# Six steps of the first group's second layer as whole fp32 products, with a new order of loads, transposes and lead-in

## Chip, core and metric

The kernel runs on one core of one Trainium2 chip. The metric is the time of one execution on the device, in microseconds (us).

## What is computed

Windowed attention with block summaries feeds a two-layer network:

```python
k_sum = k.reshape(B, H, nb, block, D).max(axis=3)      # B=4, H=8, S=768, D=64, block 32
v_sum = v.reshape(B, H, nb, block, D).mean(axis=3)
scores_l_m = np.where(mask_l, scores_l, -1e9)          # |i - j| < 16
scores_all = np.concatenate([scores_l_m, scores_s], axis=-1)
... softmax a ...
x = matmul(a, v_all)            # laid out as 3072 tokens x 512
h = x @ w_in                    # 2048 hidden units
g = h * np.tanh(softplus(h))    # Mish
out = g @ w_out                 # 3072 x 512
```

## The kernel before

**Groups and steps.** The 3072 tokens are six groups of 512 (`TG`). A group has 16 steps, one for each 128 of the 2048 hidden units, and 96 steps run one after the other. Step i multiplies `ph` = w_in x (line 425, into PSUM), ScalarE forms `a` = Mish(ph) (line 432), and two steps later `po` += a w_out (line 453), in four PSUM tiles of 128 tokens. PE does steps as ph(i), then what there is of attention, then po(i-2).

**Split operands.** x, a and both weights are fp32 values that are split into a high part rounded to fp32r (a 32-bit format that PE takes in one instruction) and a low part, the rest. Each fp32 product is three: high by high, low by high and high by low. So ph is 12 instructions of 128x512 and po another 12. The first group's `ah` is cast on ScalarE (line 441), its `al` subtracted on VectorE (line 443).

**Attention.** A chunk is 256 tokens, and a unit is one chunk of one pair of heads. The 16 turns of scores stand at the steps in the table `at` (0, 4, 8, 12, 15, 19, ...), with two units each. A turn runs over several steps: scores (`sc`, line 330) at its step; row minima and masks on VectorE (`pr`, `nm`, line 352), exps on ScalarE (line 356), reciprocals on VectorE and the multiplication on GpSimd (POOL, line 370) at the next; transposes on PE (`pt_ps`, line 378) at the end of the step after that, with ScalarE's copies (`pt`, line 380); and the products with the values (`x_ps`, line 410) at the next turn. From the turn at step 15 on, the transposes are VectorE's (line 391). VectorE also takes the block maxima of the keys (`km`, line 255, from `ks`) and the block sums of the values (`vq`, line 283, from `vsum`). `ks` and `vsum` share one buffer, so each is loaded when the one before has been reduced.

**Weights.** w_in and w_out reach the core as 16 pieces of two steps each, in the order w_in 0, w_in 2, w_out 0, w_in 4, w_out 2, w_in 6, ... , w_in 14, w_out 12, w_out 14 (a piece is named by its first step, and the order listing prints w_8 for both w_in's and w_out's). They come as 64-bit numbers and are rebuilt as fp32 on the chip. A piece passes through: `load_weight` (SP's queue, two staging buffers); `begin_weight` (ScalarE forms `f`, line 140, by `rebase_weight`, in some steps later than the rest; VectorE forms `x`, lines 144 and 146); `join_weight` (VectorE, lines 154 and 156); `upper_weight` (ScalarE casts `w_hi`, line 164); `lower_weight` (VectorE subtracts `w_lo`, line 171). All of this happens in the lead-in and the first group. SP's queue issues loads in order, and a load whose buffer is not free holds those behind it.

**Lead-in.** Ahead of step 0 a loop over u = 0 to 10 does the attention of the first group's two chunks, a unit at a time, with the first weight pieces between.

**Order.** The program runs under a manual schedule: each engine executes its instructions in the order in which the code is written. Only semaphores tie engines together. The edits lie in the weight helpers (`home`, `begin_weight`, `join_weight`, `upper_weight`), in `ff_act`, `ff_split`, `ff_out`, in the lead-in loop and in the main loop.

## Time and profile before

| | |
|---|---|
| median of 3 runs | 637.01 us (636.95 to 637.9) |
| profiled execution | 634.93 us, span 633.1 us |
| mean granted TensorE clock | 0.987 |
| PE busy | 604.3 us (95%) |
| VectorE (DVE) busy | 384.2 us (61%) |
| ScalarE (ACT) busy | 259.6 us (41%) |
| GpSimd (POOL) busy | 75.6 us (12%) |

The span is cut from the first to the last instruction; the execution's own time is a little longer. In timelines a row gives start, duration, engine, line, operation, output and inputs with their sizes. A bracket holds the idle time ahead of it on its engine and what ended it. PE's matmul ends are modelled: a 128x512 instruction is printed with 0.39 us, but the next one starts 0.227 us later, so that an idle time in a bracket after such an instruction is 0.16 us short. SPq is SP's queue as it issues transfers.

### The profile page before, as it was taken

How to read it: one execution, taken by the hardware profiler on the slowest of the kernel's cores; microseconds unless marked ns; L12 is line 12 of the kernel's file. 1: busy time of each engine (PE TensorE's matmuls, PEld its weight loads, DVE VectorE, ACT ScalarE, POOL GpSimd, SP SyncE). 2: the span in 40 equal slices, each digit the busy share in tenths (PEclk: the TensorE clock that was granted, in tenths of full speed). 3: DMA queues.
4: the chain of work that ended last, by engine and by line, in shares of the span. 5: the costliest groups of instructions: out<-in, count | busy, mean ns of one | idle time of the engine just before them, and what ended most of it. 6: DMA issues, size and time to landing. Idle time of an engine off the chain costs nothing.

```text
span 633.1 us, 10821 instructions
## 1 busy us (share of the span) xinstructions
PE 604.3 (95%) x4104; PEld 494.1 (78%) x4104; DVE 384.2 (61%) x1032; ACT 259.6 (41%) x634; POOL 75.6 (12%) x123
## 2 busy tenths in 40 slices
PE   4768999899999999999999999999999999999997
PEld 3547877688888888788888888888888888888886
DVE  4668999884755667856646658757647536222211
ACT  3759786767245145144143253153253241111111
POOL 4441010112011011010110110110110110000000
PEclk9969999899999999999999999999999999999999
DMA  9946686633134043632033241532232110100001
GB/s 286 329 153 226 228 286 236 217 122 97 67 96 115 9 147 89 199 98 97 0 97 96 91 142 56 173 98 80 83 97 68 30 33 0 67 0 1 1 0 66
DMA packets 31779, 69.26 MB, mean 109 GB/s; under 512 B 4720, under 2 KB 11120, under 8 KB 31728
## 3 DMA queue, kind: packets, MB, share of 16 engines
q1 hardware_dynamic: 31728, 68.58, 34.2%
q8 instruction: 32, 0.52, 0.3%
q14 instruction: 19, 0.16, 0.1%
HBM read 60.16 MB, written 6.29 MB: 105 GB/s over the span
## 4 chain that ended last, share of the span: by engine, by line
PE 82%; DVE 7%; DMA 5%; issue 3%; ACT 1%; POOL 1%; SPq 1%; POOLq 0%; DVEq 0%; ACTq 0%
PE po L453 38%; PE ph L425 38%; PE x_ps L410 3%; DMA vw<-vw 3%; PE sc L330 3%; DMA w<-w_in 1%; DVE w_lo L171 1%; DVE x L144 1%; DVE x L146 1%; DMA ks<-kt 1%; DVE f L154 1%; DVE al L443 1%; DVE km L255 1%; DVE pt L391 1%; DVE pr L352 1%
## 5 line engine op out<-in xcount | busy, mean ns | idle before, releaser
L432 ACT ACTIVATE a<-ph 128x512 f32<-128x512 f32 x96 | 57.3, 597 | 283.8 <-PE ph L425 230.3
L425 PE MATMUL ph<-xh,w_hi 128*128 128x512 f32 x384 | 151.5, 395 | 1.4 <-DVE nm L352 1.4
L453 PE MATMUL po<-w_hi,ah 128*128 128x512 f32 x384 | 151.9, 396 | 0.2 <-DVE o L461 0.2
L425 PE MATMUL ph<-xh,w_lo 128*128 128x512 f32 x384 | 150.9, 393 | 0.0
L425 PE MATMUL ph<-xl,w_hi 128*128 128x512 f32 x384 | 150.8, 393 | 0.0
L453 PE MATMUL po<-w_lo,ah 128*128 128x512 f32 x384 | 149.6, 390 | 0.0
L453 PE MATMUL po<-w_hi,al 128*128 128x512 f32 x384 | 149.5, 389 | 0.0
L441 DVE CAST ah<-a 128x512 fp32r<-128x512 f32 x80 | 34.7, 434 | 144.1 <-ACT a L432 143.6
L391 DVE STREAM_TRANSPOSE pt<-pr 32x256 f32<-32x256 f32 x256 | 111.5, 436 | 3.6
L425 PEld LDWEIGHTS ph<-xh,w_hi 128*128 128x128 f32 x384 | 73.0, 190 | 17.2 <-issue 2.0
L453 PEld LDWEIGHTS po<-w_hi,ah 128*128 128x128 f32 x384 | 72.0, 188 | 18.0 <-issue 3.0
L425 PEld LDWEIGHTS ph<-xh,w_lo 128*128 128x128 f32 x384 | 72.9, 190 | 15.4
L425 PEld LDWEIGHTS ph<-xl,w_hi 128*128 128x128 f32 x384 | 72.9, 190 | 15.1
L453 PEld LDWEIGHTS po<-w_lo,ah 128*128 128x128 f32 x384 | 72.1, 188 | 15.4
L453 PEld LDWEIGHTS po<-w_hi,al 128*128 128x128 f32 x384 | 72.1, 188 | 14.4
L356 ACT ACTIVATE pr<-pr,nm 128x120 f32<-128x120 f32 x192 | 73.2, 382 | 21.1 <-DVE nm L352 20.9
L370 POOL TENSOR_TENSOR pr<-pr,rs 128x960 f32<-128x960 f32 (+1 forms) x28 | 44.0, 1573 | 227.2 <-DVE rs L367 149.1
L443 DVE TENSOR_TENSOR al<-a,ah 128x512 fp32r<-128x512 f32 x96 | 66.6, 694 | 6.5 <-ACT ah L441 3.7
L410 PEld LDWEIGHTS x_ps<-pt,vw 120*64 120x64 f32 x768 | 26.0, 143 | 17.2 <-issue 7.8
L413 DVE TENSOR_TENSOR xl<-x_ps,xh 128x512 fp32r<-128x512 f32 (+1 forms) x28 | 17.2, 614 | 36.2 <-ACT xh L412 35.8
L410 PE MATMUL x_ps<-pt,vw 120*64 120x64 f32 x768 | 29.8, 231 | 8.4 <-POOL pr L370 3.4
L356 ACT ACTIVATION_READ_ACCUMULATOR pr<-pr,nm 128x1 f32 x192 | 35.9, 187 | 0.0
(64 smaller groups left out, 451.4 us busy)
## 6 DMA issues: line engine op xcount, KB each, us to landing
qk<-qk SPq DMA_DIRECT2D x40, 496.0 KB, 4.0
vw<-vw SPq DMA_DIRECT2D x48, 192.0 KB, 5.9
w<-w_in SPq DMA_DIRECT2D x16, 512.0 KB, 3.8
w<-w_out SPq DMA_DIRECT2D x16, 512.0 KB, 4.7
ks<-kt SPq DMA_DIRECT2D x16, 384.0 KB, 4.2
out<-o SPq DMA_DIRECT2D x24, 256.0 KB, 2.3
vsum<-vs SPq DMA_DIRECT2D x12, 384.0 KB, 3.3
vw<-vm SPq DMA_DIRECT2D x40, 48.0 KB
```

The lines of the kernel that those rows point to most:

```text
L144: nc.vector.tensor_scalar(out=half[:, :, 0], in0=quarter[:, :, 1], scalar1=13, scalar2=None, op0=ALU.logical_shift_right)
L330: nc.tensor.matmul(ps[h][row, at0:at0 + KA], u["qk"][r, s, h * QT:(h + 1) * QT], u["qk"][r, s, P:], start=True, stop=True)
L356: nc.scalar.activation(pr[:, j, :], pr[:, j, :], AF.Exp, scale=-1.0, bias=nm[:, j:j + 1], accum_out=sm[:, j:j + 1])
L370: nc.gpsimd.tensor_mul(u["pr"], u["pr"], rs.unsqueeze(2).broadcast_to([P, n, KA]))
L391: nc.vector.transpose(u["tr"][b * SQ:(b + 1) * SQ, :, a * SQ:(a + 1) * SQ], u["wide"][a * SQ:(a + 1) * SQ, :, b * SQ:(b + 1) * SQ])
L410: nc.tensor.matmul(x, u["v"][:, s, d], pt, start=True, stop=True)
L413: return lambda: nc.vector.tensor_sub(xl, x, xh.bitcast(F32))
L425: nc.tensor.matmul(ph, w[:, cc * P:(cc + 1) * P], x[:, cc, :], start=(cc == 0 and n == 0), stop=(cc == NCC - 1 and n == 2))
L432: nc.scalar.activation(a, st[g, fc], AF.Mish)
L441: (nc.scalar.copy if g == 0 else nc.vector.tensor_copy)(ah, a)
L443: return lambda: nc.vector.tensor_sub(al, a, ah.bitcast(F32))
L453: nc.tensor.matmul(po[g][t], a[:, tok], w, start=(fc == 0 and n == 0), stop=(fc == NFC - 1 and n == 2))
```

## The change

- `WHOLE = 6`: in steps 0 to 5 of the first group `a` is written as fp32 and not split. `ff_out` makes one fp32 product for each of the four token tiles in place of three fp32r products, with the fp32 values of w_out pieces 0, 2 and 4.
- Those three pieces are not cast or split when they are joined, but kept, and split at the end of the first group for the later groups: the list `kept` goes to the cast's queue at step 14. Their split starts with one more ScalarE copy each.
- Lead-in: the casts at u = 8 and 10 become one at u = 9, the second split moves from u = 9 to 10, a begin with its load from u = 6 to 7, and the split, join, begin and load that stood between lead-in and step 0 are gone.
- Main loop: PE's transposes move from the end of step i+2 to step i+3, right behind its `ph`. In the first group, the key loads of a turn come one step later. Step 8 joins, begins and loads no weight piece.

```diff
--- before.py
+++ after.py
@@ -43,6 +43,7 @@
 WP = 512
 WB = 2
 SQ = 32
+WHOLE = 6
 
 
 OFFSET = 112
@@ -100,6 +101,8 @@
     weights = sorted(((w, fc) for fc in range(0, NFC, WB) for w in range(2)), key=lambda p: (p[1] + WB * p[0], p[0]))
     NW = len(weights)
     order = {piece: j for j, piece in enumerate(weights)}
+
+    whole = {order[1, fc] for fc in range(0, WHOLE, WB)}
     late = []
     split = {}
 
@@ -111,10 +114,13 @@
         pool = const if j < EARLY else late[0]
         return pool.tile([P, WB * WP], dtype, tag=f"w{part}_{j}", name=name, bufs=1)
 
+    def value_home(j, name):
+        return home(j if j in whole else min(k for k in range(j + 1, NW + 1) if k not in whole), 1, F32, name)
+
     def weight(w, part, fc):
         return split[w, fc - fc % WB, part][:, fc % WB * WP:(fc % WB + 1) * WP]
 
-    loaded, rebases, begun, joined, raised = [], [], [], [], []
+    loaded, rebases, begun, joined, raised, kept = [], [], [], [], [], []
 
     def load_weight():
         if weights:
@@ -136,7 +142,7 @@
             high = flat.bitcast(U32).rearrange("p (f two) -> p f two", two=2)[:, :, 1]
             quarter = flat.bitcast(U16).rearrange("p (f four) -> p f four", four=4)
             x = home(j, 0, U32, f"x{w}_{fc}")
-            f = home(j + 1, 1, F32, f"f{w}_{fc}")
+            f = value_home(j, f"f{w}_{fc}")
             rebases.append(lambda: nc.scalar.activation(f, high.bitcast(F32), AF.Copy, scale=2.0 ** -OFFSET))
             if not wait:
                 rebase_weight()
@@ -155,11 +161,19 @@
                                     op0=ALU.max, op1=ALU.min)
             nc.vector.scalar_tensor_tensor(out=u, in0=u, scalar=3, in1=x,
                                            op0=ALU.logical_shift_left, op1=ALU.bitwise_or)
-            joined.append((w, fc, f))
+            if order[w, fc] in whole:
+                split[w, fc, 2] = f
+                kept.append((w, fc, f))
+            else:
+                joined.append((w, fc, f))
 
     def upper_weight():
         if joined:
             w, fc, f = joined.pop(0)
+            if order[w, fc] in whole:
+                value = f
+                f = home(NW, 1, F32, f"f{w}_{fc}")
+                nc.scalar.copy(f, value)
             split[w, fc, 0] = home(order[w, fc], 0, F32R, f"w{w}_{fc}_hi")
             nc.scalar.copy(split[w, fc, 0], f)
             raised.append((w, fc, f))
@@ -428,12 +442,17 @@
 
     def ff_act(g, fc):
 
-        a = ff.tile([P, TG], F32, tag="t", name=f"a{g}_{fc}", bufs=2)
+        if g == 0 and fc < WHOLE:
+            a = ff.tile([P, TG], F32R, tag="ah", name=f"a{g}_{fc}").bitcast(F32)
+        else:
+            a = ff.tile([P, TG], F32, tag="t", name=f"a{g}_{fc}", bufs=2)
         nc.scalar.activation(a, st[g, fc], AF.Mish)
         st[g, fc] = a
 
     def ff_split(g, fc):
 
+        if g == 0 and fc < WHOLE:
+            return lambda: None
         a = st[g, fc]
         ah = ff.tile([P, TG], F32R, tag="ah", name=f"ah{g}_{fc}")
         al = ff.tile([P, TG], F32R, tag="al", name=f"al{g}_{fc}")
@@ -443,13 +462,17 @@
         return lambda: nc.vector.tensor_sub(al, a, ah.bitcast(F32))
 
     def ff_out(g, fc):
-        ah, al = st.pop((g, fc))
+        a = st.pop((g, fc))
         if fc == 0:
             po[g] = [ps_o.tile([P, DM], F32, tag="o", name=f"po{g}_{t}") for t in range(TG // P)]
-        wh, wl = (weight(1, part, fc) for part in range(2))
+        if g == 0 and fc < WHOLE:
+            products = ((a, weight(1, 2, fc)),)
+        else:
+            wh, wl = (weight(1, part, fc) for part in range(2))
+            products = ((a[0], wh), (a[1], wh), (a[0], wl))
         for t in range(TG // P):
             tok = slice(t * P, (t + 1) * P)
-            for n, (a, w) in enumerate(((ah, wh), (al, wh), (ah, wl))):
+            for n, (a, w) in enumerate(products):
                 nc.tensor.matmul(po[g][t], a[:, tok], w,
                                  start=(fc == 0 and n == 0), stop=(fc == NFC - 1 and n == 2))
             if fc == NFC - 1:
@@ -510,12 +533,13 @@
             first_key_summary(u + 1)
         if lower:
             lower()
-        if u in (3, 9):
+        if u in (3, 10):
             lower_weight()
         if u in (2, 8, 10):
             join_weight()
+        if u in (2, 9):
             upper_weight()
-        if u in (1, 6, 8, 10):
+        if u in (1, 7, 8, 10):
             begin_weight()
             load_weight()
         if u == 1:
@@ -530,12 +554,8 @@
 
     turns = sorted(at)
     values = dict(zip(turns[1:] + [turns[-1] + 4], (at[i] for i in turns)))
-    turned = {i + 2: group for i, group in at.items() if i < NFC - 1}
+    turned = {i + 3: group for i, group in at.items() if i < NFC - 1}
     following = dict(zip(turns, (at[i] for i in turns[1:])))
-    lower_weight()
-    join_weight()
-    begin_weight()
-    load_weight()
     for i in range(len(steps) + 2):
         if i - 1 in at and i < NFC:
             att_normalize(at[i - 1])
@@ -544,6 +564,8 @@
             ff_act(*steps[i])
             if i < NFC:
                 split_rest = ff_split(*steps[i])
+            if i in turned:
+                att_transpose(turned[i])
         if i - 1 in at:
             upper_weight()
             rebase_weight()
@@ -577,24 +599,31 @@
         if i in following:
             n, m = following[i]
             att_summarize_keys(*n)
-            for unit in (n, m):
-                att_load_keys(*unit)
+            if i >= NFC - 1:
+                for unit in (n, m):
+                    att_load_keys(*unit)
         if i - 1 in following:
             n, m = following[i - 1]
             if i >= NFC:
                 att_summarize_values(*n)
             if m[0] % CPB == 0:
                 load_key_source(m[0] // CPB, m[1])
+            if i < NFC:
+                for unit in (n, m):
+                    att_load_keys(*unit)
         if i - 2 in following:
             n, m = following[i - 2]
             att_summarize_keys(*m)
             for unit in (n, m):
                 att_block_keys(*unit)
+        if i == NFC - 2:
+            joined.extend(kept)
         if i not in at:
             upper_weight()
-        join_weight()
-        begin_weight(i in at)
-        load_weight()
+        if i != NFC // 2:
+            join_weight()
+            begin_weight(i in at)
+            load_weight()
         if i not in at:
             lower_weight()
         if i - 1 in at:
@@ -604,8 +633,6 @@
                 att_load_values(*unit)
         if i >= 2:
             ff_out(*steps[i - 2])
-        if i in turned:
-            att_transpose(turned[i])
 
 
 # ---- launch: one core ----
```

**Places where instructions move.** The first is ScalarE at lead-in turn u = 7, where `f_2` rebases w_out's piece, `pr_3` are the exps of the last unit, and the copies and casts feed PE. Before:

```order
L380 COPY pt_0_573<-pt_ps_0_574 120x512
L140 ACTIVATE f_2_582<-w_2_170 128x1024
L356 ACTIVATE pr_3_607,sm_3_609<-pr_3_607,nm_3_608 128x120 x4
L412 CAST xh_380<-x_ps_0_622 128x256
L380 COPY pt_1_633<-pt_ps_1_634 120x512
```

and with the change:

```order
L394 COPY pt_0_573<-pt_ps_0_574 120x512
L370 ACTIVATE pr_3_599,sm_3_601<-pr_3_599,nm_3_600 128x120 x4
L426 CAST xh_380<-x_ps_0_614 128x256
L394 COPY pt_1_625<-pt_ps_1_626 120x512
L146 ACTIVATE f_2_634<-w_2_170 128x1024
```

The exps of the last unit and the transposes' copy now stand ahead of the rebase.

The second is VectorE around step 8, where `w_8_lo` out of f_8_1115 (before) and f_8_1086 (now) is the low part of w_out's piece 8. Before, with the first row of step 8's masks last:

```order
L154 TENSOR_SCALAR f_12_1168<-f_12_1168 128x1024
L156 SCALAR_TENSOR_TENSOR f_12_1168<-f_12_1168,x_12_1167 128x1024
L144 TENSOR_SCALAR x_10_1232<-w_10_1119 128x1024
L146 TENSOR_SCALAR x_10_1232<-w_10_1119 128x1024
L171 TENSOR_TENSOR w_8_lo<-f_8_1115,w_8_hi 128x1024
L352 ISA pr_0_1308,nm_0_1309<-sc_0_0_1290,first 128x120
```

and with the change, behind the masks and `xl` of step 8:

```order
L462 TENSOR_TENSOR al_8_1172<-a_8_1169,ah_8_1171 128x512
L269 TENSOR_REDUCE km_2_1231<-ks_2_1136 128x24
L380 TENSOR_SCALAR rs_0_1253<-sm_0_1212 128x8
L381 RECIPROCAL rs_0_1253<-rs_0_1253 128x8
L297 TENSOR_REDUCE vq_2_1278<-vsum_2_1233 96x32
L298 TENSOR_SCALAR vq_2_1278<-vq_2_1278 96x32
L462 TENSOR_TENSOR al_9_1273<-a_9_1270,ah_9_1272 128x512
L160 TENSOR_SCALAR f_12_1143<-f_12_1143 128x1024
L162 SCALAR_TENSOR_TENSOR f_12_1143<-f_12_1143,x_12_1142 128x1024
L150 TENSOR_SCALAR x_10_1291<-w_10_1090 128x1024
L152 TENSOR_SCALAR x_10_1291<-w_10_1090 128x1024
L185 TENSOR_TENSOR w_8_lo<-f_8_1086,w_8_hi 128x1024
```

The low part of w_out 8 stood ahead of step 8's masks and stands at the end of step 9 now, behind `km_2`, `vq_2` and a join and a begin.

The third is VectorE at steps 10 to 14, where `w_14_lo` out of f_14_1340 (before) and f_14_1343 (now) is the low part of w_in's piece 14. Before, from step 10 to step 11:

```order
L443 TENSOR_TENSOR al_10_1438<-a_10_1435,ah_10_1437 128x512
L255 TENSOR_REDUCE km_3_1441<-ks_3_1395 128x24
L154 TENSOR_SCALAR f_12_1402<-f_12_1402 128x1024
L156 SCALAR_TENSOR_TENSOR f_12_1402<-f_12_1402,x_12_1401 128x1024
L144 TENSOR_SCALAR x_14_1451<-w_14_1343 128x1024
L146 TENSOR_SCALAR x_14_1451<-w_14_1343 128x1024
L171 TENSOR_TENSOR w_14_lo<-f_14_1340,w_14_hi 128x1024
L443 TENSOR_TENSOR al_11_1499<-a_11_1496,ah_11_1498 128x512
```

and with the change, in step 13 and the start of step 14:

```order
L381 RECIPROCAL rs_2_1523<-rs_2_1523 128x8
L462 TENSOR_TENSOR al_13_1543<-a_13_1540,ah_13_1542 128x512
L160 TENSOR_SCALAR f_14_1502<-f_14_1502 128x1024
L162 SCALAR_TENSOR_TENSOR f_14_1502<-f_14_1502,x_14_1501 128x1024
L185 TENSOR_TENSOR w_14_lo<-f_14_1343,w_14_hi 128x1024
L185 TENSOR_TENSOR w_12_lo<-f_12_1406,w_12_hi 128x1024
L462 TENSOR_TENSOR al_14_1589<-a_14_1586,ah_14_1588 128x512
```

The low part of w_in 14 stood at the end of step 11 and stands at the end of step 13 now, behind the join of w_out's piece 14.

## Rows read from the trace of the kernel before

**Rows 1.** The page, busy time of each engine, its share of the span and its instructions.

```profile
PE 604.3 (95%) x4104; PEld 494.1 (78%) x4104; DVE 384.2 (61%) x1032; ACT 259.6 (41%) x634; POOL 75.6 (12%) x123
```

**Rows 2.** Busy time in two stretches of 16 us, in the first group and in the second. Columns: stretch, its length, busy us (and instructions) of PE, PEld, DVE, ACT, POOL, granted clock, DMA share, GB/s.

```profile
64.00:80.00 16.00, 16.00 (x126) 13.12 (x125) 15.82 (x30) 12.53 (x21) 0.00 (x0) 1.00 0.70 236
...
144.00:160.00 16.00, 16.00 (x129) 13.18 (x128) 5.87 (x24) 9.56 (x25) 3.08 (x4) 1.00 0.30 97
```

**Rows 3.** The chain of work that ended last, in the second group. Columns: start, us, what.

```profile
135.55 2.72 PE po L453 x12
...
143.72 0.87 PE pt_ps L378 x8
...
148.42 0.98 PE sc L330 x32
```

**Rows 4.** The timeline of PE, its four long stops in the first group.

```profile
61.67 1.09 PE L378 MATMUL pt_ps<-ident,pr 128*120 128x128 f32 x8 [1.68 <-POOL pr L370]
...
87.92 0.87 PE L378 MATMUL pt_ps<-ident,pr 128*120 128x128 f32 x6 [1.07 <-POOL pr L370]
...
109.12 0.47 PE L425 MATMUL ph<-xh,w_hi 128*128 128x512 f32 x1 [1.45 <-DVE nm L352]
...
116.94 1.09 PE L378 MATMUL pt_ps<-ident,pr 128*120 128x128 f32 x8 [2.13 <-POOL pr L370]
```

**Rows 5.** The chain again, behind the last of these stops.

```profile
118.03 4.34 PE ph L425 x12
```

**Rows 6.** Stretches of 1 us, PE alone. Columns: stretch, length, busy us (and instructions) of PE, granted clock, DMA share, GB/s.

```profile
35.00:36.00 1.00, 0.00 (x0) 1.00 0.46 29
37.00:38.00 1.00, 0.49 (x10) 0.50 1.00 401
119.00:120.00 1.00, 1.00 (x4) 0.50 1.00 397
```

**Rows 7.** The timeline of PE at the end of the lead-in and the start of step 0.

```profile
30.84 0.69 PE L410 MATMUL x_ps<-pt,vw 120*64 120x64 f32 x16 [1.00 <-ACT pt L380]
...
37.51 1.12 PE L410 MATMUL x_ps<-pt,vw 120*64 120x64 f32 x16 [2.88 <-POOL pr L370]
38.56 1.11 PE L378 MATMUL pt_ps<-ident,pr 128*120 128x128 f32 x4
40.45 1.12 PE L410 MATMUL x_ps<-pt,vw 120*64 120x64 f32 x16 [0.78 <-POOL vw L238]
...
44.59 1.12 PE L410 MATMUL x_ps<-pt,vw 120*64 120x64 f32 x16 [1.98 <-issue]
45.65 0.80 PE L425 MATMUL ph<-xh,w_hi 128*128 128x512 f32 x1
...
50.54 1.05 PE L330 MATMUL sc<-qk 64*64 64x120 f32 x32
```

**Rows 8.** The timeline of the other engines at lead-in turn u = 7.

```profile
33.15 1.08 DVE L144 TENSOR_SCALAR x<-w 128x1024 uint16<-128x1024 uint16 x1
...
36.83 0.58 ACT L380 COPY pt<-pt_ps 120x512 f32<-120x512 f32 x1
```

**Rows 9.** Groups of instructions by line. Columns: line, engine, operation, output and inputs, count | busy us, mean ns of one | idle before, and what ended it.

```profile
L443 DVE TENSOR_TENSOR al<-a,ah 128x512 fp32r<-128x512 f32 x96 | 66.6, 694 | 6.5 <-ACT ah L441 3.7
...
L352 DVE CUSTOM_DVE_ANT_0 pr<-sc,base 128x120 f32<-128x120 f32 x128 | 31.5, 277 | 4.3 <-PE sc L330 4.3
...
L171 DVE TENSOR_TENSOR w_lo<-f,w_hi 128x1024 fp32r<-128x1024 f32 x16 | 19.5, 1216 | 0.5 <-ACT w_hi L164 0.2
...
L441 ACT CAST ah<-a 128x512 fp32r<-128x512 f32 x16 | 9.9, 620 | 0.5
```

**Rows 10.** The timeline of PE at a block-mean product (line 266): fp32 operands, 128 columns, and each product stands as two instructions; a row gathers four products that go to four 32-row parts of one PSUM tile side by side.

```profile
22.32 0.43 PE L266 MATMUL vm_ps<-vw,blocks 96*32 96x128 f32 x8 [0.33 <-ACT four L270]
22.57 0.40 PE L266 MATMUL vm_ps<-v,blocks 128*32 128x128 f32 x8
```

**Rows 11.** The timeline of SP's queue and of DVE, from a w_in load that waited for its buffer to the block maxima of keys that were loaded behind it.

```profile
86.71 0.80 SPq L124 DMA_DIRECT2D w<-w_in  x2
...
91.21 0.52 SPq L212 DMA_DIRECT2D ks<-kt  x1
...
96.33 0.95 DVE L255 TENSOR_REDUCE km<-ks 128x24 f32<-128x768 f32 x1 [1.62 <-DMA ks<-kt]
```

**Rows 12.** The page, transfers: what, count, KB each, median us from issue to landing.

```profile
vsum<-vs SPq DMA_DIRECT2D x12, 384.0 KB, 3.3
```

**Rows 13.** The timeline of DVE at steps 12 and 13: from the start of a join to the end of the begin behind it, and a block sum of values.

```profile
111.36 0.69 DVE L154 TENSOR_SCALAR f<-f 128x1024 f32<-128x1024 f32 x1
...
114.50 0.18 DVE L366 TENSOR_SCALAR rs<-sm 128x8 f32<-128x8 f32 x1
...
114.90 1.22 DVE L283 TENSOR_REDUCE vq<-vsum 96x32 f32<-96x1024 f32 x1
```

**Rows 14.** The timeline of ACT and DVE in the first steps: a step's `a`, behind which ACT casts `ah` and a `w_hi` and rebases a piece, and the first instruction of DVE behind the join of that piece.

```profile
59.99 0.60 ACT L432 ACTIVATE a<-ph 128x512 f32<-128x512 f32 x1
...
65.14 0.76 DVE L144 TENSOR_SCALAR x<-w 128x1024 uint16<-128x1024 uint16 x1
```

**Rows 15.** The timeline of DVE at the second group's second step.

```profile
162.30 3.57 DVE L391 STREAM_TRANSPOSE pt<-pr 32x256 f32<-32x256 f32 x8
165.90 1.29 DVE L461 COPY o<-po 128x512 f32<-128x512 f32 x2
```

## Prediction

> **What bounds the kernel now.** The page's first part says PE: 95% busy [rows 1]. That is a mean over unlike stages, so I read stretches next. In the second group PE is never idle and DVE works 5.87 us of 16; in the first group DVE works 15.82 of 16 [rows 2], since it rebuilds and splits the weights there. The chain of waits shows the second group as PE's work alone: 12 products of a step in 2.72 us, so 0.227 each, scores of a turn in 0.98 [rows 3]. What can be won without taking work off PE therefore lies ahead of about 130 us, and PE's own timeline shows where: four stops of 1.68, 1.07, 1.45 and 2.13 us, released by POOL or DVE [rows 4]. Each is 0.16 longer than its bracket, since a product is printed 0.39 long and the next one starts after 0.227: 7.0 in all. Behind the last one 12 products took 4.34 instead of 2.72 [rows 5], at a granted clock of 0.50 [rows 6]: 1.6 more. The lead-in holds the rest: PE waits 2.88, 0.78 and 1.98 us, its products take 1.12 where the same take 0.69 [rows 7], and the clock that goes with it is 0.50, having been 1.00 in a stretch in which PE already did nothing [rows 6].
>
> **The change, part by part** (gains negative, us, against the profiled execution's 634.93).
>
> *Lead-in.* At u = 7 DVE's `x` of a weight piece stood ahead of the last unit's masks, and ACT's rebase ahead of its exps [rows 8]; the order puts both behind. With the cast at u = 8 and 10 gone, PE waits only for POOL's product and the transposes' copy. The turn ahead had such a wait of 1.00 [rows 7], so three of some 1.0 replace 2.88 + 0.78 + 1.98 = 5.64: -2.6. If the clock then stays at 1.00, three groups of values cost 0.43 less each (1.12 against 0.69) and two of transposes about 0.45 less: -2.2; and step 0's ph takes 2.72 instead of 50.54 - 45.65 = 4.89 [rows 7]: -2.2. Sum **-7.0**, or only -2.6 if the clock falls all the same. I take the first, since the row with the wait of 1.00 shows products at full speed, and keep the second for the range.
>
> *The four stops.* DVE loses six low parts of 0.694 each [rows 9] and three of weights of 1.216 until step 16, 7.8 us in all, and ACT loses six casts of 0.620. The transposes come one step later, where POOL's product is done. Following DVE's order with these durations, it is no longer behind PE up to step 7, so all four stops and the slow stretch go: -7.0 - 1.6 = **-8.6**. The cover is DVE's slack; below is where it ends.
>
> *Whole fp32 products.* A step's po becomes 4 products, which the trace shows as two instructions each. Rows of such products: eight instructions that go to four parts side by side take 22.57 - 22.32 = 0.25, so 0.125 per instruction of 128 columns [rows 10]; eight transposes take 0.87, 0.109 each [rows 3]. For 512 columns that is 0.435 to 0.50 per instruction, 3.48 to 4.0 per step against 2.72. The lower figure comes from a stream into one part, and that is what po is: I take 0.43 and 3.45 a step, 0.73 more than now, **+4.4** over six steps. The bounds are +3.8 (0.42, if the 0.87 holds a little of the transposes' start) and +7.7 (0.50). The Trainium skill says in "FP8 and Floating Point Precision", TensorE Precision Notes, that true fp32 takes four passes through the array; four times 0.227 would give 3.63 a step, an estimate, and +5.5. It speaks against this change as the rows do: one fp32 product costs more than three fp32r ones.
>
> *A new stop at po 8.* Its third product needs w_out 8's low part, which now stands at the end of step 9 on DVE. Step 8 joins nothing, so behind its scores come eight masks at 0.2, `xl` and `al` at 0.6 and `km` at 0.9 (3.7 together, from start to start; [rows 9, 11] print each a little longer); `vsum` is loaded only once `km` has freed the shared buffer, and lands 3.3 later [rows 12]; with step 8's join gone nothing fills that time; then the block sum, 1.3 with its scaling [rows 13], `al` 0.6, join and begin 114.50 - 111.36 = 3.1 [rows 13], and `w_lo` 1.2: 13.2 in all. PE has four groups of 12 and two products to do, 11.4. So a stop of 1.8, if DVE starts step 8's masks on time. It may not: step 6's `km` waits for keys whose load now stands one step later on SP's queue, behind w_out 8's load, which waits for a staging buffer until ACT's rebase of step 5, 2.85 after ph 5 ends (the sequence of [rows 14], below, less a cast of 0.62 and a join of 1.9, and 0.2 to its start). In the kernel before, a `ks` load was issued 91.21 - 86.71 = 4.5 behind such a load and landed 5.1 later [rows 11]. With 11.4 of DVE's work between that `km` and the masks it is 23.9 from ph 5, where PE needs three po at 3.45, three ph at 2.72, and transposes, values and scores of 2.9, so 21.4, to the end of step 8's scores: 2.4 late. I take both, **+4.2** (1.0 to 4.6, since loads also land sooner). Of such stops one was followed by a clock of 0.50 [rows 4 to 6]: **+1.6** (0 to 1.6).
>
> *A new stop at ph 14.* Its third product needs w_in 14's low part, now behind w_out 14's join in step 13, and that join waits for a rebase that stands behind `a`, `ah` and a `w_hi` on ACT. The same sequence took 65.14 - 59.99 = 5.15 in the first steps [rows 14]; with `w_lo` 6.3. PE has po 11 and two products, 3.1. **+3.3** (1 to 4; the passes may run shorter there, or the masks of step 12 delay DVE).
>
> *Step 15.* The transposes now stand straight ahead of the products with the values, and these wait for ACT's `a`, `ah` (0.620) and copy (0.58) [rows 8, 9]: 2.0, of which the transposes cover 0.87: **+1.2**.
>
> *The late split.* At steps 16 and 17 ACT makes six more passes of about 1 us in time it has free; DVE's `w_lo` comes between transposes of 3.57 and po's copies [rows 15], which free PSUM tiles: **+0.5** of its 1.2 reaches PE. The changed order of the loads costs nothing by itself; the key loads are the ones that can be late, and they are in the sum above.
>
> Sum: -7.0 - 8.6 + 4.4 + 4.2 + 1.6 + 3.3 + 1.2 + 0.5 = **-0.4**, or 634.5 for that execution. The profiled execution lies 2.1 under the median; the same difference at the median gives 637.01 - 0.4 = **636.6**.
>
> **Rivals.** (1) *Loads land early, and the stop at po 8 is short.* Then it costs 1.0 instead of 4.2 and no slow stretch follows: -0.4 - 3.2 - 1.6 = -5.2, **631.8**. For it: of the four stops before I see a slow stretch behind the longest alone, and of two transfers of 384 KB one took 5.1 [rows 11], the other 3.3 in the middle [rows 12]. Against it: the wait inside step 8 is 1.8 even with everything on time.
> (2) *The clock stays down through the lead-in.* This ends slower. The place is u = 8 to 10: the new waits are no shorter than 0.78 to 1.0, and if one of them is 2 or more, as when a unit's masks are late again, the clock goes to 0.50 and stays there through ph 0, as it did here. Price 7.0 - 2.6 = 4.4: +4.0, **641.0**; with a slow stretch behind the second new stop also, 642.6. For it: PE's share of the lead-in is small. Against it: the clock was 1.00 up to a wait of 2.88 in all.
> (3) *Whole products are cheap*: each of the 48 instructions takes 0.227, as an fp32r one does. Six steps then take 10.9 instead of 16.3, -5.4 where I have +4.4: -0.4 - 9.8 = -10.2, **626.8**. The rows of such products [rows 3, 10] speak against it with nearly double that. The Trainium skill's "Perfetto Trace Analysis", Engine Utilization, has the output rate halved for FP32_LOW_HIGH; read as half for a whole product, this rival would follow from it, read as half for each instruction it agrees with the rows.
>
> **Numbers.** My forecast has 0.47; by its bounds (634.7 to 638.7 as its own range) about 0.15 of that lies over 0.2% below the median, 0.24 within it and 0.08 above. 0.2%, or 1.3 us, is what a measurement of this kernel can tell from nothing. Rival 1 has 0.26, rival 2 0.22, rival 3 0.03, and 0.02 is for none of them, half within and half above. Faster 0.15 + 0.26 + 0.03 = 0.44; same 0.24 + 0.01 = 0.25; slower 0.08 + 0.22 + 0.01 = 0.31. The range goes from 630.5 (rival 1 with products at their lower bound and a little more) to 642 (rival 2 with less than its second slow stretch); about 0.06 is left below and 0.1 above.
>
> **What would show it.** In the changed profile: products of x at u = 8 to 10 printed at 0.69 and ph 0 starting near 41 at a clock of 1.00; no stop over 1 us up to step 7; po of steps 0 to 5 as eight instructions in about 3.45; a stop of 2 to 4 inside po 8, released by `w_lo`, one of about 3 inside ph 14, released by `w_lo`, and one of about 1 ahead of step 15's values. The sum is wrong if the second group starts over 2 us earlier than before: then a new stop is missing, or the lead-in wins more. It is also wrong if the second group itself differs by more than 1 us, which no step here provides for.

## The result and the profile after

The changed kernel took 642.57 us in the median of 6 runs (641.16 to 646.44), the kernel before 636.98: a ratio of 1.0104, 95% interval 1.0069 to 1.0139. It is **slower by 1%**; the forecast was 636.6, with a range up to 642.0.

Two of the six runs took 646 us at a mean granted clock of 0.976, the rest 641 to 643 at 0.984 to 0.989, and the profiled execution is one of the two (646.44, span 644.7), 3.9 above its median, whereas that of before was 2.1 below. So the two traces differ by 11.6 us of span where the medians differ by 5.6.

The page of the kernel after, answering [rows 1], says little: PE's share is the same 95%.

```profile
PE 612.1 (95%) x4080; PEld 492.5 (76%) x4080; DVE 382.2 (59%) x1026; ACT 259.1 (40%) x631; POOL 76.3 (12%) x123
```

What it did takes PE's timeline. Three places of it follow: the lead-in, which answers to [rows 7], a whole product's step, and the stops, which answer to [rows 4].

```profile
37.64 0.98 PE L424 MATMUL x_ps<-pt,vw 120*64 120x64 f32 x16 [1.77 <-POOL pr L384]
...
40.43 1.12 PE L424 MATMUL x_ps<-pt,vw 120*64 120x64 f32 x16 [0.78 <-issue]
...
43.37 1.12 PE L424 MATMUL x_ps<-pt,vw 120*64 120x64 f32 x16 [0.78 <-POOL qk L308]
44.43 0.80 PE L439 MATMUL ph<-xh,w_hi 128*128 128x512 f32 x1
...
49.07 1.05 PE L344 MATMUL sc<-qk 64*64 64x120 f32 x32
...
55.63 3.59 PE L476 MATMUL po<-f,a 128*128 128x512 f32 x8
58.66 0.79 PE L439 MATMUL ph<-xh,w_hi 128*128 128x512 f32 x1
...
112.23 0.50 PE L476 MATMUL po<-w_hi,ah 128*128 128x512 f32 x1 [2.16 <-ACT w_hi L178]
...
118.84 0.80 PE L476 MATMUL po<-w_lo,ah 128*128 128x512 f32 x1 [5.88 <-DVE w_lo L185]
...
146.73 0.53 PE L439 MATMUL ph<-xh,w_lo 128*128 128x512 f32 x1 [3.34 <-DVE w_lo L185]
...
158.18 1.17 PE L424 MATMUL x_ps<-pt,vw 120*64 120x64 f32 x32 [0.95 <-ACT pt L394]
...
178.66 0.50 PE L476 MATMUL po<-w_hi,ah 128*128 128x512 f32 x1 [0.42 <-DVE o L484]
```

In the lead-in the first new wait is 1.77, and the products of x behind it take 0.98, 1.12 and 1.12 where 0.69 is full clock, so step 0's scores come at 49.07, only 1.5 ahead of 50.54. The eight instructions of a whole step take 58.66 - 55.63 = 3.03, and the ph behind them takes 0.42 longer than the usual 2.72, as its first product takes 0.63 to the next instead of 0.227. Between 49 and 109 PE has no stop of over 0.3, and no later one is released by POOL's product or by the masks: the four of before are gone. Then come po 8's two stops, 2.16 for the high part and 5.88 for the low part, ph 14's of 3.34, step 15's of 0.95 and a small one at the late split.

VectorE and SP's queue in steps 6 to 8 show where the wait for the low part comes from.

```profile
87.33 0.52 SPq L226 DMA_DIRECT2D ks<-kt  x1
...
87.97 0.82 SPq L303 DMA_DIRECT2D qk<-qk  x2
...
88.89 0.94 SPq L130 DMA_DIRECT2D w<-w_in  x2
...
90.81 0.95 DVE L269 TENSOR_REDUCE km<-ks 128x24 f32<-128x768 f32 x1 [4.40 <-DMA ks<-kt]
...
91.79 0.33 SPq L230 DMA_DIRECT2D vsum<-vs  x1
...
99.60 1.22 DVE L297 TENSOR_REDUCE vq<-vsum 96x32 f32<-96x1024 f32 x1 [2.90 <-DMA vsum<-vs]
...
105.22 0.27 DVE L366 CUSTOM_DVE_ANT_0 pr<-sc,first 128x120 f32<-128x120 f32 x1
```

Step 8's scores start on PE at 97.90 and end at 98.9; VectorE starts their masks at 105.22, 6.3 late. It stood idle 4.40 for `ks` and 2.90 for `vsum`, which took 99.60 - 91.79 = 7.8 to land: two `qk` loads and a w_in load, 2 MB in all, stand ahead of it on the queue.

### The profile page after: what moved, and what is told of

Same layout as the page of the kernel before. It is cut to its first block, busy times and chain, and to the rows that moved or that the text cites. A ratio compares the mean times of both kernels' runs of the same rounds, so it can differ in the third digit from the quotient of the medians.

```text
span 644.7 us, 10759 instructions
## 1 busy us (share of the span) xinstructions
PE 612.1 (95%) x4080; PEld 492.5 (76%) x4080; DVE 382.2 (59%) x1026; ACT 259.1 (40%) x631; POOL 76.3 (12%) x123
## 4 chain that ended last, share of the span: by engine, by line
PE 84%; DVE 6%; DMA 5%; issue 1%; ACT 1%; SPq 1%; POOL 0%; POOLq 0%; DVEq 0%
PE po L476 39%; PE ph L439 38%; PE x_ps L424 4%; PE sc L344 3%; DMA vsum<-vs 2%; DMA vw<-vw 1%; DMA q<-qk 1%; DVE pt L405 1%; DVE w_lo L185 1%; DVE al L462 1%; PE pt_ps L392 1%; DMA ks<-kt 1%; ACT pr L370 0%; DVE km L269 0%; DVE x L150 0%
## 5 line engine op out<-in xcount | busy, mean ns | idle before, releaser
L439 PE MATMUL ph<-xh,w_hi 128*128 128x512 f32 x384 | 153.5, 400 | 0.0
L476 PE MATMUL po<-w_lo,ah 128*128 128x512 f32 x360 | 141.3, 392 | 5.9 <-DVE w_lo L185 5.9
L476 PE MATMUL po<-w_hi,ah 128*128 128x512 f32 x360 | 143.5, 399 | 2.8 <-ACT w_hi L178 2.2
L476 PE MATMUL po<-w_hi,al 128*128 128x512 f32 x360 | 140.9, 391 | 0.0
L476 PEld LDWEIGHTS po<-w_lo,ah 128*128 128x128 f32 x360 | 68.1, 189 | 20.8 <-DVE w_lo L185 6.3
L476 PEld LDWEIGHTS po<-w_hi,ah 128*128 128x128 f32 x360 | 68.0, 189 | 20.4 <-issue 2.7
L476 PEld LDWEIGHTS po<-w_hi,al 128*128 128x128 f32 x360 | 68.1, 189 | 13.5
L462 DVE TENSOR_TENSOR al<-a,ah 128x512 fp32r<-128x512 f32 x90 | 63.6, 707 | 10.3 <-ACT ah L460 7.5
L366 DVE CUSTOM_DVE_ANT_0 pr<-sc,base 128x120 f32<-128x120 f32 x128 | 31.4, 277 | 8.0 <-PE sc L344 6.6
```

The lines of the kernel that those rows point to most:

```text
L366: nc.vector.tensor_tensor_reduce(out=pr[:, j, :], in0=ps[h][:, at0:at0 + KA], in1=m, scale=-SCALE, scalar=-NEG, op0=ALU.add, op1=ALU.min, ...
L439: nc.tensor.matmul(ph, w[:, cc * P:(cc + 1) * P], x[:, cc, :], start=(cc == 0 and n == 0), stop=(cc == NCC - 1 and n == 2))
L462: return lambda: nc.vector.tensor_sub(al, a, ah.bitcast(F32))
L476: nc.tensor.matmul(po[g][t], a[:, tok], w, start=(fc == 0 and n == 0), stop=(fc == NFC - 1 and n == 2))
```

## Experiments

All medians are of runs beside the kernel before on the same chip (635.9 to 637.0).

**again.** The changed kernel, unedited.

> The changed kernel once more, for a second profile: its executions came in two kinds, near 642 and near 646 us, and the profile I have is of the second kind (clock 0.976). Theory A (order): the stops inside po 8 (2.3 for the high part and 6.1 for the low part) and ph 14 (3.5) are made by the order of VectorE's work and stay within 1 us of these sizes; what varies is the clock in the lead-in, so that an execution near 642 shows a clock of about 0.985 and step 0's scores some 3 us earlier than 49.07. Theory B (transfers): the loads of ks and vsum vary, and an execution near 642 has a stop at po 8 that is 3 us or more shorter, with the lead-in as it was.

644.11 (641.76 to 646.09), ratio 1.0114 (1.0083 to 1.0145). The profiled run took 646.09: step 0's scores at 49.23, po 8's stops 1.63 + 5.82, ph 14's 3.31, each within 0.6 of the first profile. The stops belong to the order; *fill* below, whose clock does not fall in the lead-in, still waits 6.00 for po 8's low part and 3.31 at ph 14. The other half of theory A, what an execution near 642 looks like, came from the kernels below that have the same lead-in. Stretches of PE in this run; columns as in [rows 6]:

```profile
26.00:34.00 8.00, 5.60 (x108) 0.80 1.06 362
34.00:39.00 5.00, 3.99 (x58) 0.64 0.21 62
```

in *lowfirst*:

```profile
26.00:34.00 8.00, 4.59 (x113) 1.00 0.96 323
34.00:39.00 5.00, 2.92 (x56) 1.00 0.08 23
```

and in *keysold*:

```profile
26.00:34.00 8.00, 5.71 (x106) 0.79 1.02 336
34.00:39.00 5.00, 2.53 (x40) 1.00 0.08 27
```

From 26 to 34 us the clock was 0.80 here and 1.00 in *lowfirst*, under the same program up to that point. But *keysold* had 0.79 there too, and its step 0's scores came at 46.63, near the 45.82 of *lowfirst* and the 46.67 of *two*. What goes with late scores is the stretch from 34 to 39: 0.64 here and 0.84 in the first profile, against 1.00 in *lowfirst* and *keysold* and 0.97 in *two*. In *lowfirst* the clock fell all the same, later, behind two short waits (PE's timeline):

```profile
38.40 0.69 PE L424 MATMUL x_ps<-pt,vw 120*64 120x64 f32 x16 [0.78 <-issue]
...
40.74 1.12 PE L424 MATMUL x_ps<-pt,vw 120*64 120x64 f32 x16 [0.78 <-POOL vw L252]
```

**oldlead.** The weight calls of the lead-in as before, so that every piece comes a step earlier.

```diff
-        if u in (3, 10):
+        if u in (3, 9):
             lower_weight()
...
-        if u in (2, 9):
+        if u in (2, 8, 10):
             upper_weight()
-        if u in (1, 7, 8, 10):
+        if u in (1, 6, 8, 10):
...
+    lower_weight()
+    join_weight()
+    begin_weight()
+    load_weight()
     for i in range(len(steps) + 2):
```

> The changed kernel with the lead-in's weight calls as they were before (the begin at u = 6, the casts at 8 and 10, the split at 9, and the split, join, begin and load ahead of step 0). Every weight piece then stands one step earlier: w_out 8's low part at the end of step 7, ahead of step 8's masks, and w_in 14's low part in step 11. Theory A (the dropped begin and load put every piece a step later, and that makes both new stops): both go with their slow stretches, 10.6 and 5.2 us; the lead-in loses the 1.5 it had won; 646.4 - 15.8 + 1.5 = 632 against that profile, 629 to 632 in the median. Theory B (loads come late and DVE is late at step 8 whatever the order of the pieces): the stop turns up at step 8's masks or at al instead, and the median stays at 636 or above.

638.89, ratio 1.0023 (1.0004 to 1.0042): the time is theory B's. Both stops named are gone, but PE now stops in po 12, for both parts of its weights (PE's timeline):

```profile
141.15 0.50 PE L476 MATMUL po<-w_hi,ah 128*128 128x512 f32 x1 [2.57 <-ACT w_hi L178]
...
142.99 0.69 PE L476 MATMUL po<-w_lo,ah 128*128 128x512 f32 x1 [1.10 <-DVE w_lo L185]
```

The skipped step 8 is missed there, as the next run shows. Theory A had the cause of the two stops, not the sum.

**oldlead_noskip.** The same, and step 8 works on a piece.

```diff
-        if i != NFC // 2:
-            join_weight()
-            begin_weight(i in at)
-            load_weight()
+        join_weight()
+        begin_weight(i in at)
+        load_weight()
```

> As the kernel with the old lead-in calls (638.9), and step 8 joins, begins and loads a piece again. There the waits for vsum leave VectorE 3.1 to 4.0 idle and it is late at ph 14 (2.7) and po 12 (1.3 and a slow stretch). Theory A (the skipped step is what VectorE misses later): w_in 14's low part stands a step earlier and the join fills the wait at step 8; both stops and the slow stretch go, -5.9: 633. Theory B (VectorE's work and its waits for loads are the bound, in whatever order): the stop moves, 637 or above.

632.80, ratio 0.9953 (0.9929 to 0.9977): as theory A had it. Left are step 15's stop and 1.1 us inside step 12's scores, which wait for POOL's copy into a late `qk`.

**lowfirst.** The split ahead of the join in steps 9 and 13.

```diff
+        if i in (9, 13):
+            lower_weight()
         if i != NFC // 2:
             join_weight()
...
-        if i - 1 in at:
+        if i - 1 in at and i not in (9, 13):
             lower_weight()
```

> The changed kernel with one edit: at steps 9 and 13 the split of a piece's low part stands ahead of the join and begin of the next piece, instead of behind them. Theory A: po 8 gets its low part 3.1 us earlier (stop 6.1 to 3.0; the 2.3 for the high part stay, since ScalarE makes it), ph 14 gets its own 3.1 earlier or as soon as ScalarE has the high part (stop 3.5 to about 0.5), and the slow stretch behind ph 14's stop (1.7) goes: -8, so 634 to 635. Theory B (VectorE's order does not matter, the pieces or sums arrive late): less than 3 us, 639 or above.

639.37, ratio 1.0047 (1.0027 to 1.0068): the time is theory B's, just. PE's stops, from its timeline:

```profile
109.24 0.80 PE L476 MATMUL po<-w_hi,ah 128*128 128x512 f32 x1 [2.42 <-ACT w_hi L178]
...
112.58 0.80 PE L476 MATMUL po<-w_lo,ah 128*128 128x512 f32 x1 [2.12 <-DVE w_lo L185]
...
129.74 0.50 PE L476 MATMUL po<-w_lo,ah 128*128 128x512 f32 x1 [1.33 <-DVE w_lo L185]
...
139.72 0.50 PE L439 MATMUL ph<-xh,w_lo 128*128 128x512 f32 x1 [1.53 <-DVE w_lo L185]
```

Po 8's low part came 3.0 sooner, 17.9 behind the start of step 8's scores instead of 20.9, as theory A said. But ph 14 keeps 1.53, and po 10 stops for 1.33 where it had not: part of what one stop gives back, the next takes.

**keysold.** The turns' key loads where they were.

```diff
-            if i >= NFC - 1:
-                for unit in (n, m):
-                    att_load_keys(*unit)
+            for unit in (n, m):
+                att_load_keys(*unit)
...
-            if i < NFC:
-                for unit in (n, m):
-                    att_load_keys(*unit)
```

> The changed kernel with one edit: a turn's two key loads (qk) are issued at the turn's step again and not a step later. In the profile qk's two loads and a w_in load stand on SP's queue between ks and vsum of step 6, vsum takes 7.8 us to land and the block sum waits 2.9 for it. Theory A (order, with the key loads as one part of it): vsum lands in 3 to 5, VectorE reaches step 8's masks about 3 earlier, and po 8's stop falls from 8.4 to 5 to 6; median -3, about 639.5. Theory B (weights' lag alone): ks then waits longer instead, within 1 us of 642.6.

640.84, ratio 1.0067 (1.0045 to 1.0088): theory A, with less gained than its 3. SP's queue and VectorE in steps 6 to 8:

```profile
83.78 0.52 SPq L226 DMA_DIRECT2D ks<-kt  x1
...
88.32 0.95 DVE L269 TENSOR_REDUCE km<-ks 128x24 f32<-128x768 f32 x1 [4.31 <-DMA ks<-kt]
...
89.30 0.33 SPq L230 DMA_DIRECT2D vsum<-vs  x1
...
94.06 1.20 DVE L297 TENSOR_REDUCE vq<-vsum 96x32 f32<-96x1024 f32 x1
...
99.65 0.27 DVE L366 CUSTOM_DVE_ANT_0 pr<-sc,first 128x120 f32<-128x120 f32 x1
```

and PE's timeline in po 8:

```profile
113.23 0.67 PE L476 MATMUL po<-w_lo,ah 128*128 128x512 f32 x1 [5.12 <-DVE w_lo L185]
```

`vsum` lands within 4.8 and VectorE does not wait for it; the masks start 11.3 behind `km`, not 14.4. `ks` is as late as ever (4.31). Po 8 lost 7.0 over its usual time, ph 10 nothing, where they lost 10.6 together. So the moved key loads are 3.6 of what po 8 costs.

**two.** `ks` in a buffer of its own (one that a late weight piece uses afterwards).

```diff
-        ks = sources[b, hp, 0] = stage.tile([P, S], F32, tag="sum", ...)
+        ks = sources[b, hp, 0] = (home(NW - 1, 0, F32, f"ks{b}_{hp}")[:, :S] if b == 1 else
+                                  stage.tile([P, S], F32, tag="sum", ...))
```

> The changed kernel with one edit: in the first group the keys for the block maxima (ks) have a buffer of their own, where ks and vsum took turns in one; the order of SP's queue is untouched. In the changed kernel VectorE stands idle 4.4, 2.9 and 3.2 us ahead of km of step 6 and of the block sums of steps 7 and 9. Theory A (the loads behind one buffer put VectorE late, which makes po 8's stop): vsum is issued 2 us earlier in step 6 and 3 or more earlier in step 8, so VectorE splits w_out 8 about 5 earlier, and the stop of 8.4 falls to 3 to 4; median 636 to 638. Theory B (the transfers themselves are slow, or ks decides alone): less than 1.5 us, 641 or above.

642.07, ratio 1.0084 (1.0050 to 1.0117): theory B. `vsum` of step 6 on SP's queue, and its block sum on VectorE:

```profile
85.44 1.02 SPq L304 DMA_DIRECT2D qk<-qk  x2
...
87.47 0.42 SPq L231 DMA_DIRECT2D vsum<-vs  x1
...
96.47 1.22 DVE L298 TENSOR_REDUCE vq<-vsum 96x32 f32<-96x1024 f32 x1 [2.15 <-DMA vsum<-vs]
```

`vsum` is issued ahead of `km` (88.39) and takes 9.0 to land. From the issue of the `qk` loads to the block sum it is 96.47 - 85.44 = 11.0 us here and 99.60 - 87.97 = 11.6 in the first profile, though `vsum` is issued 2.0 behind them here and 3.8 there. It was not the shared buffer that held it, but the bytes ahead of it on the queue.

**wholeonly.** Whole products alone: the kernel before with `WHOLE = 6`, `kept` and their split, and none of the new order.

> The kernel before with one part of the change: the first six steps' second layer on whole fp32 operands, split at the group's end; loads, transposes and lead-in as before. Theory A (the new order is what costs): +4.4 for the products and +0.5 for the late split, and of the four stops (8.6) at least 4 go, as VectorE has 7.8 us less to do by step 6: 633.5 to 638, likeliest 635.5. Theory B (whole products are a loss in themselves, the stops are POOL's and stay): 641.

630.25, ratio **0.9909** (0.9882 to 0.9935): theory A, and better than the range it gave. All four stops of before go, and no new one comes. Busy times in stretches from step 0's scores on; columns as in [rows 2].

```profile
50.30:76.30 26.00, 26.00 (x180) 17.52 (x180) 22.67 (x58) 21.85 (x50) 2.27 (x3) 1.00 0.80 283
76.30:99.10 22.80, 22.80 (x113) 14.78 (x111) 17.73 (x25) 14.49 (x20) 2.56 (x3) 1.00 0.76 258
99.10:124.00 24.90, 24.90 (x170) 20.59 (x168) 23.96 (x46) 18.54 (x36) 3.66 (x3) 1.00 0.70 224
124.00:150.00 26.00, 26.00 (x205) 21.44 (x201) 16.05 (x51) 20.44 (x51) 3.00 (x5) 1.00 0.37 114
```

PE is busy throughout the first group, at a clock of 1.00. The transposes at the end of step i+2 do no harm once VectorE is not late.

**turn3.** Only the transposes' new place, on the kernel before.

```diff
-    turned = {i + 2: group for i, group in at.items() if i < NFC - 1}
+    turned = {i + 3: group for i, group in at.items() if i < NFC - 1}
...
             if i < NFC:
                 split_rest = ff_split(*steps[i])
+            if i in turned:
+                att_transpose(turned[i])
...
-        if i in turned:
-            att_transpose(turned[i])
```

> The kernel before with one part of the change: PE's transposes in step i+3 behind its ph, not at the end of step i+2; all operands split as before. Theory A (three of the four stops are PE waiting for POOL, and there the product is done a step later): 1.84, 1.23 and 2.29 us and the slow stretch of 1.6 go, step 15 costs 1.2: -5.7, 631.3. Theory B (VectorE is the bound of the first group, POOL's lateness only shows it): the stops turn up at al or w_lo, and the median stays within 2 us of before.

636.92, ratio 1.0014 (0.9989 to 1.0038): theory B. POOL's stops are gone, but products with the values wait for ScalarE's copy instead, and the masks' stop stays (PE's timeline):

```profile
71.53 1.18 PE L424 MATMUL x_ps<-pt,vw 120*64 120x64 f32 x32 [0.87 <-ACT pt L394]
...
108.91 0.47 PE L439 MATMUL ph<-xh,w_hi 128*128 128x512 f32 x1 [1.56 <-DVE nm L366]
...
126.81 1.98 PE L424 MATMUL x_ps<-pt,vw 120*64 120x64 f32 x32 [2.60 <-ACT pt L394]
```

**whole0.** The new order alone (`WHOLE = 0` in the changed kernel).

> The changed kernel with all operands split as before (WHOLE = 0): the new order alone. Theory A (the order is the loss, whole products are a gain that depends on VectorE): PE saves 4.4 for the products and 0.7 for the late split, but VectorE has 7.8 us more to do by step 6 and reaches step 8 later still; the stop at po 8 grows by 8 to 12: 645 to 650. Theory B (whole products are the loss): 637 or below.

646.61, ratio 1.0163 (1.0120 to 1.0206): the time theory A gave, but not in its place. The weight pieces that come a step late stop PE at once, for both parts in po 0 and again in po 4 (PE's timeline); po 8 stops for 3.96:

```profile
55.19 0.80 PE L476 MATMUL po<-w_hi,ah 128*128 128x512 f32 x1 [2.66 <-ACT w_hi L178]
...
60.61 0.80 PE L476 MATMUL po<-w_lo,ah 128*128 128x512 f32 x1 [4.19 <-DVE w_lo L185]
...
90.67 0.50 PE L476 MATMUL po<-w_lo,ah 128*128 128x512 f32 x1 [2.74 <-DVE w_lo L185]
```

**fill.** Spare work for PE in the lead-in.

```diff
             att_scores([todo[u]])
+        if 4 <= u <= 10:
+            spare = ps_w.tile([P, 512], F32, tag="w", name=f"spare{u}")
+            for j in range(4):
+                nc.tensor.matmul(spare[:, j * P:(j + 1) * P], ident, ident, start=True, stop=True)
```

> The changed kernel with four spare products of 128x128 (ident by ident, read by nobody) on PE behind the scores' place at each lead-in turn u = 4 to 10, where PE waits 0.8 to 1.8 us. They do 0.9 us of work a turn at full clock. Theory A (the clock falls because PE stands still in the lead-in): it stays at 1.00 through ph 0, step 0's scores come at about 44 where they came at 49.1 and 49.2 (clock down from 27 on) or 45.8 to 46.7 (down from 40 on) in runs of this lead-in; no execution near 646, median 638 to 640. Theory B (the clock falls for another reason, or the chain through VectorE and GpSimd sets the pace): the spare products only add to PE's work, 642 to 646.

639.60 (638.97 to 640.41), ratio 1.0055 (1.0034 to 1.0075): theory A, and no run near 646.

Stretches of PE, columns as in [rows 6]:

```profile
26.00:34.00 8.00, 7.43 (x134) 1.00 0.66 225
...
39.00:44.00 5.00, 5.00 (x40) 1.00 0.75 258
```

and its timeline from step 0's first product to its scores:

```profile
40.99 0.50 PE L439 MATMUL ph<-xh,w_hi 128*128 128x512 f32 x1
...
44.13 0.62 PE L344 MATMUL sc<-qk 64*64 64x120 f32 x13
```

Step 0 begins at 40.99 and its ph takes 3.1, its scores come at 44.13. The clock stayed at 1.00 throughout.

**best** and **bestfill.** *Wholeonly* with the new lead-in calls and, ahead of step 0, a join, a begin and a load; then with the spare products.

```diff
-        if u in (3, 9):
+        if u in (3, 10):
             lower_weight()
...
             join_weight()
+        if u in (2, 9):
             upper_weight()
-        if u in (1, 6, 8, 10):
+        if u in (1, 7, 8, 10):
...
-    lower_weight()
     join_weight()
```

> The kernel before with whole products (630.25) and the changed kernel's lead-in calls, but with a join, a begin and a load ahead of step 0, so that the pieces stay as early as before. Theory A: step 0's scores come at 45.8 to 46.7 instead of 50.3 where the clock holds, or at 49 where it falls early: -1.3 to -4.5, 626 to 629, and no new stop up to the second group. Theory B (the pieces' work moved behind step 0 is missed by VectorE): a stop at po 2 to ph 4, 630 or above.

> The same with the spare products at lead-in turns u = 4 to 10. Theory A (PE's clock in the lead-in): step 0's scores at about 44, 2 to 5 us ahead of the same without them: 623 to 626. Theory B: no gain, within 1 us of it or slower.

630.56, ratio 0.9917 (0.9885 to 0.9948), and 628.95, ratio **0.9896** (0.9863 to 0.9930). In *best* the scores of step 0 come at 46.38, 3.9 ahead of *wholeonly*, and 3.0 of it is gone 7 us later, since PE's third ph waits for a buffer until ScalarE has read an earlier one. ScalarE was late with that, since it had stood idle for a w_out load whose rebase comes first (ScalarE's timeline, then PE's):

```profile
50.06 1.15 ACT L146 ACTIVATE f<-w 128x1024 f32<-128x1024 f32 x1 [5.37 <-DMA w<-w_out]
...
53.17 0.50 PE L439 MATMUL ph<-xh,w_hi 128*128 128x512 f32 x1 [2.80 <-ACT a L449]
```

In *wholeonly* that rebase started at 49.09. So the lead-in runs ahead of a load that comes no sooner, and step 4's scores come at 71.05 where *wholeonly* has 71.25. The time is theory B's on *best*, but the stop is at ph 2 and is ScalarE's, not VectorE's. On *bestfill* neither theory holds: the clock was 1.00 from 26 to 50 us, but step 0's scores came at 45.80, not 44, the same ph waits 2.95, and step 4's scores are 0.4 ahead of *best*. The medians are 1.6 apart, and the intervals overlap. Both versions beat both kernels; whether *bestfill* beats *wholeonly* the intervals leave open.

## Why the prediction was wrong

Terms of the sum, against what the two traces measure (profile after less profile before):

| term | forecast | measured |
|---|---|---|
| lead-in to step 0's scores | -7.0 | -1.5 (-3.9 to -4.7 in *lowfirst*, *keysold* and *two*) |
| four stops and slow stretch | -8.6 | -8.6 |
| whole products | +4.4 | 6 x (3.03 + 0.42 - 2.72) = +4.4 |
| po 8, with its slow stretch | +5.8 | (5.05 + 11.01) - 2 x 2.72 = +10.6 |
| ph 14 | +3.3 | 7.94 - 2.72 = +5.2 |
| step 15 | +1.2 | 1.98 - 0.79 = +1.2 |
| late split | +0.5 | +0.7 |
| sum | -0.4 | +12.0 (span: +11.6) |

(Each time is from the start of a group of products to the start of the next, less the same group's unhindered time.)

**What held.** The whole product's price, from rows of other fp32 products; that it came out to the hundredth is partly luck, since the rows allowed 0.42 to 0.50 for an instruction. Further the end of the four stops; the place and releaser of the stops that I named, and the chains inside: from step 8's masks to w_out 8's split 118.84 - 105.22 = 13.6 where I had 13.2, ph 14's wait 3.5 where I had 3.3. The stop for po 8's high part I had not seen coming; it adds nothing, since the low part comes later still.

**What failed, first: the lead-in's full clock.** I took it because a wait of about 1 us had been seen at full clock. The waits came out about as I had them, 1.77, 0.78 and 0.78 in the first profile and 1.30, 0.78 and 0.78 in *lowfirst*, and the clock fell all the same, between 38 and 42 us, in most profiles with this lead-in also for a while between 26 and 34. This was rival 2's mechanism at rival 2's place, without the wait of 2 or more that it named: its 0.22 was too little. *Fill* shows it: with PE kept busy the clock stays, step 0's scores come at 44.13, and the forecast's 43.5 (50.54 - 7.0) is nearly met. The median is 3 us lower with it. That rival 2's 642.6 is the measured median is luck: it counts the third point below, but has the lead-in at -2.6 and nothing of the second.

**Second: how late VectorE is at step 8.** I had 2.4, it was 6.3. The `ks` load was issued 87.33 - 77.32 = 10.0 behind ph 5's end, not 7.35, and landed in 3.5, not 5.1; that is +1.1. The rest is the 2.90 that VectorE stood idle for `vsum`: I let it land within the 3 us that other work covers, because its median was 3.3 [rows 12], and did not carry the moved key loads to the queue it shares with them. *Keysold* gives these 3 us back on VectorE; *two* shows that the shared buffer is not what holds it. I had costed the key loads' move only for what is loaded behind the weights, and the order of the loads at nothing.

**Third: the slow stretch behind ph 14**, 1.7, which I gave to po 8 alone. The trace shows most products after 146.73 at 0.43 from start to start.

**What the median hides.** The terms as measured belong to one execution of 646.44. With the lead-in of *lowfirst*, *keysold* or *two* the same sum is 2.4 to 3.2 lower, which is most of the 3.9 by which that execution lies above its median. Why the clock comes back for 34 to 39 us in one execution and not in another stays open, and so does the 2.1 by which the profiled execution of before lies below its own.

**The change taken apart.** In the old order whole products gain 0.9%; in the new order they seem to gain 0.6% (646.6 to 642.6), with intervals that overlap. The new order loses 1.6% without them. Taking its parts back one after the other gave 642.6, 638.9 (lead-in calls), 632.8 (step 8), 630.25 (transposes and key loads, taken back together). Each of these steps gave time back in this order; on the kernel before, the transposes' place alone cost nothing clear of noise (*turn3*), and lead-in calls that keep the pieces early cost nothing either (*best*). What costs is that weight pieces or loads come later, and VectorE has no slack for that in the first group: the 7.8 us that whole products free there were stood out again, waiting. VectorE's idle stretches of over 0.3 us, from step 0's scores to step 15, add up to 9.7 us before and 25.2 after. I had followed this slack up to step 7 and called it the cover; its end was where I said, and twice as deep.

## What to carry to other kernels

Here the work that the change freed on the full engine paid only where the same change did not push loads and weight pieces back: follow each moved load into the queue, with the bytes ahead of it, and not the buffer alone. Price a product of another kind from the nearest rows of that kind: here that term held. Where PE is idle in short pieces, a gain that is counted at full clock needs a row that shows the clock through the whole stretch, not one wait in it.

## What the runs showed of the hardware

- Spare products in a lead-in that leaves PE idle kept the granted clock at 1.00 (*fill*) and brought the whole kernel some 3 us; without them the same lead-in had 0.60 from 26 to 34 us in the first profile, 0.80 in *again*, 0.79 in *keysold* and 1.00 in *lowfirst*.
- A 384 KB load landed within 4.8 us behind 1 MB on SP's queue (*keysold*), and in 7.8 and 9.0 behind 2 MB (the first profile and *two*).
- An fp32 product of 128x512 stands as two instructions, 0.43 us each with what it costs the instruction behind it: 3.45 for four. The Trainium skill's four passes ("FP8 and Floating Point Precision", TensorE Precision Notes) would give 3.63 by four times 0.227, an estimate; the trace is near it, and below.
